# Attention tile: where the sink columns are transposed and copied, and the order of logits and natural transposes

## The chip, the core and the metric

The kernel runs on one core of one Trainium2 chip. The metric is the device time of one execution in microseconds (us). A core has five engines that work at the same time, each through its own list of instructions in order: TensorE (PE; its weight loads are shown apart as PEld), VectorE (DVE), ScalarE (ACT), GpSimd (POOL) and SyncE (SP, which here only issues DMA transfers). An instruction that needs another engine's result waits for that engine's semaphore, and everything behind it in its own list waits too. Operands lie in SBUF; matmuls write to PSUM, eight banks of 2 KB for each of 128 partitions.

## The reference

Attention with a window of 128 keys and 4 sink keys over 4 batches, 8 heads, 768 positions and 64 elements a head; its output, 3072 tokens of 512 elements, goes through a mixture of 16 experts (4 groups of 4, one expert a token).

```python
def _attn_ref(q, k, v, n_sink, window):
    scores = scale * np.matmul(q, k.transpose(0, 1, 3, 2))
    keep = is_sink | in_window          # pos < 4, or 0 <= row - col < 128
    scores = np.where(keep, scores, -1000000000.0)
    scores = scores - np.max(scores, axis=-1, keepdims=True)
    a = np.exp(scores)
    a = a / (np.sum(a, axis=-1, keepdims=True) + 1e-09)
    return np.matmul(a, v)

def _moe_ref(x, w_group, w_expert, w1, w2):
    # per token: group by argmax, then expert of that group by argmax
    h = np.maximum(xg[mask_e] @ w1[g, e], 0.0)
    ye = h @ w2[g, e]
    out[tok_idx] = (g_w * e_w)[:, None] * ye
```

## The kernel before

The 3072 rows are cut into 24 tiles of 128 rows (6 tiles for each of 4 batches); all 8 heads of a tile are worked together. One loop (`for i in range(NI + 2)`) runs the tiles as a pipeline three deep. Cycle `i` does for tile `i` the scores, row maxima and exponentials; for tile `a = i - 1` the transposes of the exponentials, their copies to SBUF, masks, and the product with the values; for tile `b = i - 2` the logits of the router, the transposes back to natural row order, the normalisation (`norm`) and the store of the attention output. After the loop the experts run: gathered rows, two matmul layers, scatter. What fills the gaps of the loop is weight preparation (`whi`, `wlo`) and the routing arithmetic on DVE.

The order on each engine is the order in which the code calls the engine (every call is pinned in program order), so moving a line of the loop moves its instructions on each engine.

The steps that matter here, with the tile names that a profile row shows as `out<-in`:

- `scores(i, 0)` and `scores(i, 1)`: PE writes `ps`, four heads each.
- `trans(a)`: 16 PE transposes of the exponentials, `tp<-ident,pt`, into both banks of the pair `tp`.
- `sink_t(a)`: two PE transposes of the 96 sink columns (4 sinks of 8 heads in three pieces, made by POOL as `sp`), `lg<-ident,sp` and `po<-ident,sp`: they go to the first 64 columns of the two banks `ob[0]` (named lg) and `ob[1]` (named po).
- `evac(a, 0)`, `evac(a, 1)`: ACT copies the two halves of `tp` to SBUF, `pa<-tp`; for every tile that is not the first of its batch POOL then makes two masked versions of each half (`pu<-pa`, `pa<-pa`).
- `sink_evac(a)`: ACT casts the two pieces of transposed sinks, `spT<-lg` and `spT<-po`.
- `maxima(i, g)` on DVE (`sm<-ps,msk`), `exps(i, g)` on ACT (`pt<-sm,st`), four heads each.
- `logits(b)`: PE, `lg<-wsd,xT`; `natural(b)`: 8 PE transposes, `tp<-ident,xT`, into the first half of both `tp` banks; `norm(b)`: DVE, `xt<-tp,rc`.
- `values(a, 0)`, `values(a, 1)`, `sink_values(a)`: PE accumulates into `po` (`po<-pu,vv`, `po<-pa,vv`, `po<-spT,svp`); `out_evac(a)`: ACT copies it, `xT<-po`.

`tp` is one pair of banks for the whole loop (`bufs=1`), so the transposes of cycle `i + 1` wait until `norm(b)` of cycle `i` has read it.

Of the kernel before, what the change touches and what calls it, by code (L numbers as in the profile page):

```python
# [22 lines left out]
B, H, S, D = 4, 8, 768, 64  # L23
# [5 lines left out]
NDC = DM // P  # L29
# [100 lines left out]
def moe_attention(tc, kqT, vN, vS, nsw, wgx, w1, w2, out):  # L130
    nc = Pinned(tc)
    v = nc.vector
    with ExitStack() as top, ExitStack() as att:
# [15 lines left out]
        def const(shape, dt, name):  # L149
            return cp.tile(shape, dt, name=name)  # L150
# [17 lines left out]
        vts, svs, env, bat = {}, {}, {}, {}  # L168
# [4 lines left out]
        def pair():  # L173
            return ps_p.tile([P, 2, 4 * P], F32, name="tp")
# [55 lines left out]
        ident = const([P, P], F32, "ident")  # L230
# [106 lines left out]
        def put_gates(n):  # L337
            for _ in range(min(n, len(gates))):
                t, g = gates.pop(0)
                nc.sync.dma_start(xd[t * P:(t + 1) * P, DM:XW], g)  # L340
# [292 lines left out]
        def gather(r, j):  # L633
            w = min(P, CAPT[r] - j * P)
            cc = BASE[r] + j
            xg[r, j] = t = gp.tile([P, XW], F32, name="xg")
            src = xd[0:sum(BATCHES[:(SNAP if j < EC else SNAPB) + 1]) * P] if r == 0 else xd
            nc.gpsimd.indirect_dma_start(
                out=t[0:w], out_offset=None, in_=src,
                in_offset=bass.IndirectOffsetOnAxis(ap=gidx[0:w, cc:cc + 1], axis=0))  # L640
# [8 lines left out]
        def dve(us):  # L649
            state["dve"] = max(state["dve"], state["clk"]) + us  # L650
# [3 lines left out]
        def prefetch(depth):  # L654
            while len(raws) < depth and state["issued"] < len(chunks):
                l, r, c = chunks[state["issued"]]
                if (f"id{r}" if r < 2 else "eid") not in ready:
                    return
                state["issued"] += 1
                if r not in regs:  # L660
                    src = (eidi if r > 1 else eid01)[0:1, r:r + 1]
                    regs[r] = nc.nc.values_load(src, engines=[ENG.SP], min_val=0, max_val=NE - 1)
                e = bass.ds(regs[r], 1)
                rw = raw()[:, 0:F]
                if l == 1:
                    nc.sync.dma_start(rw, w1[e, c * P:(c + 1) * P, :].rearrange("o p f -> (o p) f"))
                else:
                    nc.sync.dma_start(rw.rearrange("p (k n) -> p k n", k=2),
                                      w2[e, 2 * c * P:(2 * c + 2) * P, :].rearrange("o (k p) n -> p (o k) n", p=P))
                state["dma"] = max(state["dma"], state["clk"] + DMALAG) + DMATIME  # L670
                raws.append((l, r, c, rw, state["dma"] + DMASLACK))

        def wjob(force=False):
            if tail:
                prefetch(RAW)
            k = state["done"]
            if raws and not force and state["clk"] < raws[0][4]:
                return None
            if not raws or k >= state["freed"] + WBUF or (k % WBUF >= WA and len(wpool) < 2):
                return None  # L680
            l, r, c, rw, _ = raws.pop(0)
            wp = wpool[k % WBUF >= WA]
            hi = wp.tile([P, F], F32R, name="whi")
            lo = wp.tile([P, F], F32R, name="wlo")
            z = F if tail else F // 2
            nc.scalar.copy(hi[:, 0:z], rw[:, 0:z])

            def rest():
                v.tensor_tensor(lo, rw, hi.bitcast(F32), ALU.subtract)
                wt[l, r, c] = hi, lo  # L690
                if tail:
                    prefetch(RAW)
            dve(1.2)
            state["done"] += 1
            if tail:
                rest()
                return True

            def more():
                nc.scalar.copy(hi[:, z:], rw[:, z:])  # L700
                return rest

            half.append(more)
            return None

        psb = [ps_s.tile([P, 4, 256], F32, name=f"ps{g}") for g in range(2)]
        ob = [ps_a.tile([P, DM], F32, name=n) for n in ("lg", "po")]
# [74 lines left out]
        def sink_t(i):  # L782
            sp = env[i]["sp"].rearrange("p a h k -> p (a h k)").bitcast(F32)
            for f in range(2):
                r = slice(f * D, (f + 1) * D)
                nc.tensor.transpose(ob[f][0:96, 0:D], sp[r], ident[r, r])

        def sink_evac(i):
            env[i]["spT"] = spT = wk.tile([96, P], F32R, name="spT", bufs=2)
            for f in range(2):  # L790
                nc.scalar.copy(spT[:, f * D:(f + 1) * D], ob[f][0:96, 0:D])

        po = ob[1].rearrange("p (c n) -> p c n", c=HP)
        lg = ob[0][:, D:D + 2 * H * PW].rearrange("p (t n) -> p t n", t=2)
# [25 lines left out]
        def natural(i):  # L820
            for c in range(NDC):
                for j in range(2):
                    r = slice(j * D, (j + 1) * D)
                    nc.tensor.transpose(env["tp"][:, j, c * D:(c + 1) * D], env[i]["xT"][r, c], ident[r, r])

        def logits(i):
            xT = env[i]["xT"]
            for c in range(NDC):
                for g in range(2):
                    r = slice(g * D, (g + 1) * D)  # L830
                    nc.tensor.matmul(lg[r, i % 2, 2 * c * PW:2 * (c + 1) * PW], xT[:, c, r],
                                     wsd[:, c].rearrange("p j n -> p (j n)"), start=True, stop=True)
# [247 lines left out]
        for i in range(NI + 2):  # L1080
            live = i < NI
            a, b = i - 1, i - 2
            mid, old = 0 <= a < NI, 0 <= b < NI
            state["clk"] += 3.0
            if i == NI:
                state.update(gap=0.0, dve=state["clk"])
                sps.close()
                put_gates(MAXB)
                while later:
                    gather(*later.pop(0))  # L1090
                ps_h = fl.enter_context(tc.tile_pool(name="ps_h", bufs=4, space=PSUM, side="right", reuse_waits="tile"))
                tail.append(ps_h)
                next(ew)
                next(ew)
                if half:
                    half.pop()()()
            if live:
                load_v(i)
            if live:
                scores(i, 0)  # L1100
                if i == 1:
                    scores(i, 1)
            if mid or old:
                env["tp"] = pair()
            if mid:
                trans(a)
                sink_t(a)
                evac(a, 0)
                sink_evac(a)
                evac(a, 1)  # L1110
            late = None
            if live:
                if i != 1:
                    scores(i, 1)
                issue()
                warm(FILL[i] if i < len(FILL) else 0, ob[0][:, 224:416])
                late = half.pop()() if half else wjob()
            if live:
                maxima(i, 0)
                exps(i, 0)  # L1120
            else:
                routing(TSTEP, (None,))
                next(ew, None)
            if old:
                logits(b)
                natural(b)
            if live:
                maxima(i, 1)
                exps(i, 1)
                sink_split(i)  # L1130
            if i == 0:
                late_consts()
            if i % NT == (4 if i else 0) and i < NI - NT + (not i):
                split_s((i + 2) // NT)
            state["clk"] += 3.0
            if old:
                norm(b)
            routing(1, ("pe",))
            if old:
                norm_logits(b)  # L1140
            if late:
                late()
            if mid:
                values(a, 0)
                values(a, 1)
                sink_values(a)
                out_evac(a)
            if later and not gates:
                gather(*later.pop(0))
            put_gates(2 if live else MAXB)  # L1150
            routing((REND if i < NI - 1 else 2) if live else TSTEP, (None, "rd"))
            if live and i % 2:
                sums(i)
            if i >= CHOOK and (i % 2 == 0 or i > NI - 4):
                prefetch(min(RAW, len(raws) + (1 if live else RAW)))
            if not live:
                wjob()
                next(ew, None)
# [48 lines left out]
        with tc.If(fv > 0), ExitStack() as fv_pool:  # L1207
            tp = fv_pool.enter_context(tc.tile_pool(name="tabw", bufs=1))
# [233 lines left out]
```

## Time and profile before

| | us |
|---|---|
| median of 3 runs | 518.01 (516.5 to 519.64) |
| the profiled execution | 516.01 |
| its span, first to last instruction | 514.2 |
| busy on DVE, ACT, POOL | 381.9 (74%), 345.1 (67%), 158.8 (31%) |
| 24 executions of `xT<-po` (end of a tile's values) | from 16.3 to 166.2 |

The granted TensorE clock is 0.997 of full speed over the span. The attention loop lies between about 6 and 170 us of the span, the experts behind it. Rows of the view of instructions in order of time read: start (us), length (us), engine, line (here always a recording helper's, L100), operation, out<-in, shape, xcount of merged instructions, and in brackets the engine's idle time before the row and what ended it. Matmuls overlap, so a group's share of PE is the distance from its start to the next group's start, not its length.

### The profile page before, as it was taken

Reading aid. Unit: us, or ns where it says so; the run is one execution under the profiler, and the core shown is the slowest. Engines: PE = TensorE matmul, PEld = TensorE weight load, DVE = VectorE, ACT = ScalarE, POOL = GpSimd, SP = SyncE. Lnnn points to the kernel's source line nnn. Section 1 sums busy time; section 2 is a strip of 40 time slices with the busy share of each in tenths; the row PEclk is TensorE's granted clock in tenths of the full one; section 3 lists DMA queues with packets and bytes.
Section 4 is the critical chain, followed back from the end, with each engine's and each line's share of the span. In section 5 each row is a group of like instructions: output and inputs, shape, how many; then the busy total and the mean of one; then the engine's idle time right before and its main releaser. Section 6 shows DMA issues by size and latency. Waiting matters only on the chain. (4 is left out here: it accounts for less than half of the span.)

```text
span 514.2 us, 14708 instructions
## 1 busy us (share of the span) xinstructions
PE 498.3 (97%) x5399; PEld 418.1 (81%) x5399; DVE 381.9 (74%) x1183; ACT 345.1 (67%) x901; POOL 158.8 (31%) x272
## 2 busy tenths in 40 slices
PE   7999999999899999999999999999999999999994
PEld 5788888878678888989889878787779788988884
DVE  7566986987996889984175668946988887788840
ACT  4888887888875345772274677745877887688631
POOL 3454462453465012423304013121243033202201
PEclk9999999999999999999999999999999999999998
DMA  7777877687786545896239488859878896779200
GB/s 199 245 212 215 235 213 221 216 320 212 221 291 153 181 123 205 303 319 227 67 92 319 130 267 313 277 163 297 283 246 307 305 319 226 263 244 321 93 24 27
DMA packets 50000, 114.33 MB, mean 222 GB/s; under 512 B 9486, under 2 KB 9486, under 8 KB 49920
## 3 DMA queue, kind: packets, MB, share of 16 engines
q1 hardware_dynamic: 45424, 99.96, 60.3%
q0 software_dynamic: 4352, 13.06, 7.2%
q8 instruction: 44, 0.72, 0.6%
q10 hardware_dynamic: 144, 0.29, 0.3%
q14 instruction: 36, 0.29, 0.2%
HBM read 100.69 MB, written 13.05 MB: 221 GB/s over the span
## 5 line engine op out<-in xcount | busy, mean ns | idle before, releaser
L100 DVE TENSOR_TENSOR wlo<-rw,whi 128x1024 fp32r<-128x1024 f32 x128 | 153.2, 1219 | 36.4 <-ACT whi L100 36.1
L100 PE MATMUL po<-whi,un 128*128 128x512 f32 (+3 forms) x448 | 149.2, 393 | 0.0
L100 ACT CAST whi<-rw 128x1024 fp32r<-128x1024 f32 (+1 forms) x132 | 131.7, 1023 | 18.2 <-DMA rw<-in_w 15.2
L100 PE MATMUL ph<-un,whi 128*128 128x256 f32 (+4 forms) x576 | 132.2, 317 | 1.1 <-DVE un L100 0.6
L100 POOL DMA_INDIRECT out<-ot,sidx x33 | 45.5, 1380 | 236.0 <-ACT ot L100 142.3
L100 PE MATMUL po<-wlo,un 128*128 128x512 f32 (+4 forms) x264 | 101.6, 390 | 0.0
L100 PE MATMUL ph<-un,wlo 128*128 128x160 f32 (+4 forms) x416 | 100.6, 267 | 0.0
L100 PEld LDWEIGHTS po<-whi,un 128*128 128x128 f32 (+2 forms) x448 | 79.9, 179 | 23.6
L100 PEld LDWEIGHTS ph<-un,whi 128*128 128x128 f32 x576 | 94.8, 189 | 3.5 <-DVE hc L100 1.0
L100 ACT ACTIVATE pt<-sm,st 128x136 f32<-128x136 f32 x192 | 75.8, 407 | 9.8 <-DVE st L100 9.8
L100 PEld LDWEIGHTS ph<-un,wlo 128*128 128x128 f32 x416 | 77.2, 189 | 0.8
L100 PEld LDWEIGHTS po<-wlo,un 128*128 128x128 f32 (+3 forms) x264 | 43.5, 165 | 13.2
L100 DVE CUSTOM_DVE_ANT_0 sm<-ps,msk 128x136 f32<-128x136 f32 x192 | 45.9, 295 | 6.7 <-PE ps L100 2.2
L100 PE MATMUL ps<-kb,qb 64*64 64x216 f32 (+1 forms) x768 | 44.7, 351 | 2.0 <-DMA qb<-in_kqT 2.0
L100 POOL DMA_INDIRECT xg<-xd,gidx x33 | 35.0, 1061 | 32.9 <-DVE idz L100 20.9
L100 ACT ACTIVATE ot<-po,cg 128x512 f32<-128x512 f32 (+4 forms) x33 | 22.5, 681 | 31.6 <-PE po L100 22.7
L100 DVE TENSOR_TENSOR hc<-ph,hc 128x160 f32<-128x160 f32 (+2 forms) x64 | 22.1, 346 | 23.4 <-ACT hc L100 23.3
L100 ACT ACTIVATE un<-ph 128x256 fp32r<-128x256 f32 (+1 forms) x40 | 15.7, 395 | 34.2 <-PE ph L100 33.7
L100 ACT COPY pa<-tp 128x512 f32<-128x512 f32 x48 | 28.5, 593 | 15.0 <-PE po L100 13.6
L100 ACT ACTIVATION_READ_ACCUMULATOR pt<-sm,st 128x1 f32 x192 | 38.2, 199 | 0.0
L100 POOL TENSOR_SCALAR_AFFINE_SELECT pu<-pa 64x512 f32<-64x512 f32 x40 | 26.4, 660 | 22.0 <-ACT pa L100 18.1
L100 ACT COPY hc<-ph 128x160 f32<-128x160 f32 (+2 forms) x64 | 19.8, 311 | 19.2 <-PE ph L100 11.8
(190 smaller groups left out, 723.8 us busy)
## 6 DMA issues: line engine op xcount, KB each, us to landing
rw<-in_w SPq DMA_DIRECT2D x128, 512.0 KB, 4.9
vv<-in_vN SPq DMA_DIRECT2D x24, 512.0 KB, 5.0
kb<-in_kqT SPq DMA_DIRECT2D x23, 288.0 KB, 4.6
qb<-in_kqT SPq DMA_DIRECT2D x24, 256.0 KB, 4.0
xd<-xt SPq DMA_DIRECT2D x24, 256.0 KB, 3.9
svr<-in_vS SPq DMA_DIRECT2D x4, 192.0 KB, 4.9
xg<-xd,gidx POOLq DMA_INDIRECT x33, 4.5
out<-ot,sidx POOLq DMA_INDIRECT x33, 5.0
```

The costliest lines, as they stand in the source:

```text
L100: r = f(*a, **k)
```

## The change

The two sink transposes leave their place behind `trans(a)` and go behind `scores(i, 1)`; they write columns 256 to 319 of the two `tp` banks and not `lg` and `po`. One cast takes both pieces from there, and it stands on ACT between `exps(i, 0)` and `exps(i, 1)`. `natural(b)` and `logits(b)` change places, and both move ahead of `maxima(i, 0)` in the code, so that on PE they stand directly behind the sink transposes (nothing of `maxima` or `exps` is on PE).

```diff
         def sink_t(i):
@@
-                nc.tensor.transpose(ob[f][0:96, 0:D], sp[r], ident[r, r])
+                nc.tensor.transpose(env["tp"][0:96, f, NDC * D:(NDC + 1) * D], sp[r], ident[r, r])

         def sink_evac(i):
             env[i]["spT"] = spT = wk.tile([96, P], F32R, name="spT", bufs=2)
-            for f in range(2):
-                nc.scalar.copy(spT[:, f * D:(f + 1) * D], ob[f][0:96, 0:D])
+            nc.scalar.copy(spT.rearrange("p (f q) -> p f q", f=2), env["tp"][0:96, :, NDC * D:(NDC + 1) * D])
@@
             if mid:
                 trans(a)
-                sink_t(a)
                 evac(a, 0)
-                sink_evac(a)
                 evac(a, 1)
@@
                 late = half.pop()() if half else wjob()
+            if mid:
+                sink_t(a)
+            if old:
+                natural(b)
+                logits(b)
             if live:
                 maxima(i, 0)
                 exps(i, 0)
             else:
                 routing(TSTEP, (None,))
                 next(ew, None)
-            if old:
-                logits(b)
-                natural(b)
+            if mid:
+                sink_evac(a)
             if live:
                 maxima(i, 1)
                 exps(i, 1)
```

On PE, one cycle from the steady part of the loop (`-` is before, `+` now):

```order
 L100 MATMUL ps_195<-kb,qb 64x216 x8
 L100 MATMUL tp<-ident,pt 128x64 x16
-L100 MATMUL lg<-ident,sp 96x64
-L100 MATMUL po<-ident,sp 96x64
 L100 MATMUL ps_196<-kb,qb 64x216 x8
-L100 MATMUL lg<-wsd,xT 64x40 x8
-L100 MATMUL tp<-ident,xT 128x64 x8
+L100 MATMUL tp<-ident,sp 96x64 x2
+L100 MATMUL tp<-ident,xT 128x64 x8
+L100 MATMUL lg<-wsd,xT 64x40 x8
 L100 MATMUL po<-pu_109,vv 64x64 x8
 L100 MATMUL po<-pa,vv 64x64 x8
```

The sink transposes now stand next to the natural transposes, and the logits next to the values.

On ACT, the same cycle before, from one copy of a finished tile to the exponentials:

```order
L100 COPY xT<-po 128x512
L100 COPY pa<-tp 128x2x4x64
L100 CAST spT<-lg 96x64
L100 CAST spT<-po 96x64
L100 COPY pa<-tp 128x2x4x64
L100 ACTIVATE pt,st<-sm,st 128x2x68 x8
```

And now, the same stretch:

```order
L100 COPY xT<-po 128x512
L100 COPY pa<-tp 128x2x4x64 x2
L100 ACTIVATE pt,st<-sm,st 128x2x68 x4
L100 CAST spT<-tp 96x128
L100 ACTIVATE pt,st<-sm,st 128x2x68 x4
```

The two casts that stood between the two copies are one cast, behind four of the eight exponentials.

On DVE, around `norm(b)` in a cycle of the same part, with what each instruction waits for:

```order
 L100 ISA sm,st<-ps_196,msk 128x136
 L100 ISA st 128x1
-L100 TENSOR_TENSOR xt<-tp,rc 128x2x4x64 [waits DMAHW7_49,PE_49,Activation_49]
-L100 TENSOR_TENSOR lw<-lg,rc 128x320
+L100 TENSOR_TENSOR xt<-tp,rc 128x2x4x64 [waits DMAHW7_49,Activation_49]
+L100 TENSOR_TENSOR lw<-lg,rc 128x320 [waits PE_49]
 L100 TENSOR_REDUCE lt<-lw 128x40 [waits DVE_49]
```

No DVE instruction has moved, but `norm(b)` now waits for ACT alone (an ACT instruction that itself comes behind the natural transposes: the cast), and the product with the logits waits for PE on its own.

## The prediction

> **What bounds the kernel now.** I read the page first, then the stretches of the attention loop and of the experts, then one steady cycle on each engine, and last the waits within the loop.
>
> ```profile
> span 514.2 us, 14708 instructions
> PE 498.3 (97%) x5399; PEld 418.1 (81%) x5399; DVE 381.9 (74%) x1183; ACT 345.1 (67%) x901; POOL 158.8 (31%) x272
> ...
> 10.00:158.20 148.20, 144.20 (x3185) 116.76 (x3173) 118.46 (x589) 122.50 (x507) 73.53 (x185) 1.00 0.77 235
> ```
>
> The last line is the loop: its length, then the busy time of PE, PEld, DVE, ACT and POOL. PE is busy for 144.2 of 148.2 us, and nearly all the time behind it, so a shift of PE's stream in the loop reaches the end almost whole. But "busy" hides how the cycle is held. Here is one steady cycle (tile 10) on PE:
>
> ```profile
> 66.71 0.71 PE L100 MATMUL tp<-ident,pt 64*128 64x64 f32 x16
> 67.25 0.22 PE L100 MATMUL lg<-ident,sp 64*96 64x64 f32 x1
> ...
> 67.40 0.96 PE L100 MATMUL ps<-kb,qb 64*64 64x216 f32 x16
> 68.29 0.67 PE L100 MATMUL lg<-wsd,xT 128*64 128x40 f32 x16
> 68.89 0.46 PE L100 MATMUL tp<-ident,xT 64*128 64x64 f32 x8
> 69.28 0.69 PE L100 MATMUL po<-pu,vv 128*64 128x64 f32 x16
> 69.80 0.64 PE L100 MATMUL po<-pa,vv 128*64 128x64 f32 x16
> 70.26 0.66 PE L100 MATMUL po<-pu,vv 128*64 128x64 f32 x16
> 70.95 0.69 PE L100 MATMUL po<-pa,vv 128*64 128x64 f32 x16
> 71.57 0.66 PE L100 MATMUL po<-spT,svp 96*128 96x128 f32 x4
> ```
>
> From start to start: transposes 0.54, sinks 0.15, scores 0.89, logits 0.60, natural transposes 0.39, then values 0.52, 0.46, 0.69, 0.62. The third block of values takes 0.69 where its like takes 0.46: PE waits there about 0.2 for the last mask. POOL makes the four masks in a row as soon as ACT has copied the first half:
>
> ```profile
> 67.54 0.59 ACT L100 COPY pa<-tp 128x512 f32<-128x512 f32 x1 [0.97 <-PE po L100]
> 68.02 0.21 ACT L100 CAST spT<-lg 96x64 fp32r<-96x64 f32 x1
> ...
> 68.23 0.60 ACT L100 COPY pa<-tp 128x512 f32<-128x512 f32 x1
> ...
> 68.19 0.65 POOL L100 TENSOR_SCALAR_AFFINE_SELECT pu<-pa 64x512 f32<-64x512 f32 x1 [1.91 <-ACT pa L100]
> ...
> 70.25 0.65 POOL L100 TENSOR_SCALAR_AFFINE_SELECT pa<-pa 64x512 f32<-64x512 f32 x1
> ...
> PEld po L100 <- POOL pa L100: 2.1, 12, 0.2
> ```
>
> The first mask begins when the first copy ends (67.54 + 0.59), the fourth ends at 70.90, and PE goes on at 70.95. The last line counts the waits of this kind in the loop: 12, together 2.1 us. So in 12 of the cycles the ring transposes, first copy, masks, last values, next transposes sets the pace, with PE 0.2 us ahead of it; elsewhere it is PE alone (first tiles of a batch, which have no masks, and cycles with routing matmuls ahead of the values).
>
> **The change part by part, on PE.** Without the sinks behind the transposes, the second scores start 0.06 earlier (67.34), and the sinks could start at 67.34 + 0.89 = 68.23. They write the `tp` banks, so they wait for both copies out of them. The second copy takes the place of the first cast, 68.02, and ends at 68.62. How soon PE resumes is shown where the logits wait for a cast:
>
> ```profile
> 81.01 0.21 ACT L100 CAST spT<-lg 96x64 fp32r<-96x64 f32 x1
> ...
> 81.27 0.32 PE L100 MATMUL lg<-wsd,xT 128*64 128x40 f32 x4 [0.15 <-ACT spT L100]
> ```
>
> That is 0.05 after the cast's end at 81.22. So the sinks start at 68.67, with PE idle for 0.44, a wait that the logits filled before. These rows show another thing: the logits waited for a cast out of other columns of the same bank, so bank neighbours are kept apart. The Trainium skill ("PSUM — Partial Sum Buffer", PSUM bank collisions raise a hardware error) says that any two engines, two readers too, are to be kept apart by bank and not by address; the trace agrees (the 0.05 above). By addresses alone `norm` would not wait for the cast, and my sum below would be about 1.2 lower (no delay in cycles 7, 13 and 19).
>
> From the sinks on: sinks and natural transposes with the switch behind them 0.06 + 0.18 + 0.15 = 0.39, logits 0.44 without their switch (0.60 - 0.16), 0.05 into the values, which follow with no switch between: values at 69.55, against 69.28, **0.27 later**. With no switch ahead, the first block takes 0.47: the fourth block is ready at 69.55 + 3 x 0.47 = 70.96. The masks allow it at 70.95. In the 12 cycles the old wait for the mask just covers the new one for the copy: I count **0 for each**, between -0.05 (the fourth block starts without a restart) and +0.11. The upper end is a second copy that begins when the first has ended (0.59 behind its start) and not 0.48 behind it, as the cast does; the trace has no two such copies in a row, and I take the cast's row as the nearest.
>
> The switches: a group of another tile shape costs 0.15 (behind 64-column work) to 0.27 (behind scores) at its start against 0.05 within a shape. The change has one switch fewer a cycle. The Trainium skill ("TensorEngine Tiling (Array Packing)", Key Properties) says that changing the tiling mode drains the array; the rows agree. If that were all, every cycle would gain about 0.13; that is a rival below.
>
> **Cycles without cover.** Cycle 2 gains. There the sinks held PE for POOL's pieces:
>
> ```profile
> 16.23 0.71 PE L100 MATMUL tp<-ident,pt 64*128 64x64 f32 x16
> 17.18 0.26 PE L100 MATMUL lg<-ident,sp 64*96 64x64 f32 x1 [0.24 <-POOL sp L100]
> ...
> 19.85 0.69 PE L100 MATMUL po<-pu,vv 128*64 128x64 f32 x16
> ```
>
> Now the scores start at 16.87, the dummy matmuls at 17.76, the sinks at 18.36, when both copies are done; values at 18.36 + 0.88 = 19.24, 0.61 earlier, and 0.05 more without the switch. Cycle 1 loses 0.08, since its sinks' values wait for the cast behind four exponentials. Together **-0.6**.
>
> Cycles 11 and 18 have routing matmuls between transposes and values, so the masks are done in time:
>
> ```profile
> 73.05 0.71 PE L100 MATMUL tp<-ident,pt 64*128 64x64 f32 x16
> ...
> 75.63 0.88 PE L100 MATMUL lg<-af,bf 128*128 128x112 f32 x6
> 76.43 0.69 PE L100 MATMUL po<-pu,vv 128*64 128x64 f32 x16
> ```
>
> Sinks at 73.05 + 1.96 = 75.01, logits done by 75.84, a switch 0.16, routing 0.80: values at 76.80 for 76.43, 0.37 each, **+0.7**.
>
> **The cast behind the exponentials.** It is queued on ACT behind four exponentials, and `norm` on DVE waits for it. Behind `norm` on DVE stand the routing and the next maxima. In cycle 7 the fifth exponential begins at 52.06; without the two casts ahead (0.21) the new cast starts at 51.85 and, costed between the 0.21 of a 96x64 cast and the 0.59 of a 128x512 copy, near the small one, takes 0.26: `norm` at 52.16.
>
> ```profile
> 51.79 0.69 DVE L100 TENSOR_TENSOR xt<-tp,rc 128x512 f32<-128x512 f32 x1
> ...
> 52.06 0.41 ACT L100 ACTIVATE pt<-sm,st 128x136 f32<-128x136 f32 x1
> ...
> 58.58 0.39 ACT L100 ACTIVATE pt<-sm,st 128x136 f32<-128x136 f32 x1
> ...
> 58.88 0.66 PE L100 MATMUL po<-spT,svp 96*128 96x128 f32 x4
> ```
>
> That is 0.38 late, and DVE has no gap from there to the maxima of cycle 8. So the fifth exponential of cycle 8 moves from 58.58 to 58.96, its cast ends at 59.22, and the sinks' values start at 59.27 for 58.88: +0.39 for cycles 7 and 8 (the switch path alone gives 0.27). Cycles 13 and 14 are built alike, +0.3. Together **+0.7**. In steady cycles DVE has room and the same delay costs nothing.
>
> Cycles 19 to 21 are the worst, since a weight copy (0.52) stands ahead of the exponentials:
>
> ```profile
> 127.91 0.68 DVE L100 TENSOR_TENSOR xt<-tp,rc 128x512 f32<-128x512 f32 x1
> ...
> 128.82 0.40 ACT L100 ACTIVATE pt<-sm,st 128x136 f32<-128x136 f32 x1
> ...
> 127.50:141.40 13.90, 13.06 (x60) 1.00 0.76 235
> ...
> 139.47 1.15 POOL L100 DMA_INDIRECT xg<-xd,gidx  x1 [0.87 <-DVE ps L100]
> ...
> 141.37 0.69 PE L100 MATMUL po<-pu,vv 128*64 128x64 f32 x16 [0.58 <-POOL pu L100]
> ```
>
> The cast ends at 128.82 - 0.21 + 0.26 = 128.87, `norm` starts at 128.92 and not 127.91: 1.0 later. The third line is DVE alone: busy for 13.06 of 13.90 us, so nothing takes the delay up. The gather on POOL waits for DVE's work (or the store behind it), and the masks and PE wait for the gather: **+1.0**, with 0 as the lower end if the gather hangs on something earlier. PE's own losses up to there (0.3 to 0.6) vanish in that wait.
>
> **The end of the loop.** In cycle 24 PE waits for the second copy as well, while the expert work that it did meanwhile comes later: +0.25. In cycle 25 the natural transposes come ahead of an expert block, so `norm` no longer waits 0.40, and PE's later wait of 0.80 for DVE shrinks with it:
>
> ```profile
> 170.04 0.69 DVE L100 TENSOR_TENSOR xt<-tp,rc 128x512 f32<-128x512 f32 x1 [0.40 <-PE tp L100]
> ...
> 175.29 0.66 PE L100 MATMUL ph<-ident,xg 128*128 128x128 f32 x4 [0.80 <-DVE un L100]
> ```
>
> Together **-0.1**. Sum: -0.6 + 0.7 + 0.7 + 1.0 - 0.1 = **+1.7 us**. The profiled execution took 516.01, 1.8 more than its span and 2.0 below the median of 518.01; it would become 517.7, and the median **519.7**.
>
> **The rivals.**
> 1. Slower: the second copy comes later than I count. The 12 covered cycles have no slack left (70.96 against 70.95), so each 0.1 us between the copies' end and the sinks costs there at once, and in the 4 uncovered ones too. At 0.2 us (0.11 for copies that do not overlap, the rest in the resumption) that is 16 x 0.2 = 3.2: 522.9. For it: nothing in the trace shows the pair of copies; against it: the cast follows a copy at 0.48.
> 2. The DVE delay is taken up: the gather does not depend on `norm`. Then 518.7.
> 3. Faster: the switches alone count, since the copies end in time. Four uncovered cycles gain 0.13 each and not 0.3, the sinks' stalls for POOL (six waits before) go, about -3.0 in all: 515.0. Against it stands the row of the second copy: it would have to end 0.4 us earlier. By the skill's tiling page alone this would be the outcome.
>
> **How the numbers follow.** My forecast has 0.55, rival 2 0.13, rival 1 0.25, rival 3 0.07. Less than 0.5% (2.6 us) can't be told from no change here. Forecast and rival 2 lie within it; of the forecast a sixth of its chance falls above it, since 519.7 is near the bound of 520.6. That gives faster 0.06, same 0.60, slower 0.34. The range: the low end takes the 12 cycles at -0.05 (-0.6), no DVE term (-1.0), and the 1.5 by which runs lie below their median: 516.6; the high end is rival 1 with a little of the spread: 523.2.
>
> **What would show it.** Right: sinks 1.9 to 2.0 us behind the start of the transposes, behind a PE gap of about 0.4; the 12 waits for masks nearly gone; cycles of the steady part still 6.35 long; `norm` waiting for ACT, by about 1 us where a weight copy stands ahead. Wrong: steady cycles of 6.5 or more (rival 1), or below 6.3 (rival 3), or the tile-21 values at the old distance from tile 19 (rival 2).

## The result, and the profile after

The changed kernel took 523.39 us (median of 4 runs, 521.77 to 524.16) beside 517.25 us for the kernel before on the same chip: a ratio of 1.0107, with a 95% interval of 1.0063 to 1.0151. Measured once more beside others (first experiment below) it took 519.99 for 517.49, ratio 1.0062 [1.0027, 1.0096]. It is slower, by 0.6 to 1.1%. The forecast was 519.7, slower by 0.3%, with a range up to 523.2: the first median lies 0.2 us above that range, the second within it. The medians are of all executions and the ratios leave out the few in a slower state, and a ratio is not the quotient of the two medians beside it (519.99 / 517.49 is 1.0048).

The head of the page after, to be read against the one before:

```profile
span 520.1 us, 14651 instructions
PE 494.1 (95%) x5399; PEld 416.0 (80%) x5399; DVE 382.4 (74%) x1183; ACT 343.3 (66%) x877; POOL 158.4 (30%) x272
```

The span grew by 5.9 us while PE's busy time fell by 4.2: the work did not grow, PE waits more. The view by stretches shows the loop again (length, busy time of PE, PEld, DVE, ACT, POOL, then the granted clock):

```profile
10.00:165.20 155.20, 140.75 (x3185) 114.87 (x3174) 118.75 (x587) 121.41 (x483) 75.57 (x185) 0.99 0.74 225
```

It is 7.0 us longer than before's 148.2, and PE is idle in it for 14.4 us and not for 4.0. The view of what the engines waited for in the loop (us in total, times, longest):

```profile
DVE xt L100 <- ACT spT L100: 11.5, 18, 1.3
PE tp L100 <- ACT pa L100: 10.6, 21, 1.1
...
PE ps L100 <- issue: 1.7, 1, 1.7
...
PEld po L100 <- POOL pa L100: 0.3, 2, 0.2
```

The first line is `norm` waiting for the cast, as foreseen, the second PE's new wait for the second copy. The third is a stall for which the profile has no releaser. The last is what is left of the twelve waits for masks, 2.1 us before. PE's groups and the copies of one steady cycle (tile 10) after, in order of time:

```profile
67.35 0.71 PE L100 MATMUL tp<-ident,pt 64*128 64x64 f32 x16
67.99 0.96 PE L100 MATMUL ps<-kb,qb 64*64 64x216 f32 x16
68.18 1.07 ACT L100 COPY pa<-tp 128x512 f32<-128x512 f32 x2 [0.97 <-PE tp L100]
69.40 0.26 PE L100 MATMUL tp<-ident,sp 64*96 64x64 f32 x2 [0.45 <-ACT pa L100]
69.47 0.44 PE L100 MATMUL tp<-ident,xT 64*128 64x64 f32 x8
69.84 0.67 PE L100 MATMUL lg<-wsd,xT 128*64 128x40 f32 x16
70.33 0.66 PE L100 MATMUL po<-pu,vv 128*64 128x64 f32 x16
...
71.76 0.64 PE L100 MATMUL po<-pa,vv 128*64 128x64 f32 x16
...
73.81 0.71 PE L100 MATMUL tp<-ident,pt 64*128 64x64 f32 x16
```

Both copies end at 68.18 + 1.07 = 69.25, as costed (the second 0.48 behind the first). But the sinks begin at 69.40, 0.15 behind that and not 0.05, and 2.05 behind the transposes and not 1.96. The values begin 2.98 behind the transposes; I had 2.84, before had 2.57. From the sinks to the values PE takes 0.93, where sinks, logits and natural transposes took 0.15 + 0.60 + 0.39 = 1.14 before: the switch of tile shape that the change saves is there. The cycle is 6.46 long and was 6.34. The prediction had named 6.35 as the sign of its being right and 6.5 or more as that of rival 1; this lies between the two, nearer to rival 1.

The stall without a releaser is in cycle 15, first on PE, then in stretches of 2 us:

```profile
105.82 0.76 PE L100 MATMUL ps<-kb,qb 64*64 64x216 f32 x9
108.31 0.89 PE L100 MATMUL ps<-kb,qb 64*64 64x216 f32 x7 [1.74 <-issue]
109.13 1.12 PE L100 MATMUL tp<-ident,pt 64*128 64x64 f32 x16
```

```profile
106.00:108.00 2.00, 0.58 (x9) 0.16 (x5) 1.46 (x9) 0.57 (x1) 0.12 (x1) 1.00 0.92 332
108.00:110.00 2.00, 1.69 (x23) 1.07 (x23) 0.72 (x4) 0.00 (x0) 0.00 (x0) 0.62 0.75 293
110.00:112.00 2.00, 2.00 (x28) 1.03 (x24) 0.71 (x9) 1.63 (x4) 0.90 (x2) 0.53 0.02 8
```

PE stands still for 1.74 us amid one group of matmuls whose operands were there for the ones before it; behind that the granted clock is 0.62 and 0.53 in two stretches of 2 us (from 108.5 to 111.9 it is 0.50), so the next transposes take 1.12 for 0.71. My prediction had no such term.

### The profile page after: what moved, and what is told of

It reads as the page before. It is cut to its first block, busy times and chain, and to the rows that moved or that the text cites. A ratio compares the mean times of both kernels' runs of the same rounds, so it can differ in the third digit from the quotient of the medians.

```text
span 520.1 us, 14651 instructions
## 1 busy us (share of the span) xinstructions
PE 494.1 (95%) x5399; PEld 416.0 (80%) x5399; DVE 382.4 (74%) x1183; ACT 343.3 (66%) x877; POOL 158.4 (30%) x272
## 3 DMA queue, kind: packets, MB, share of 16 engines
HBM read 100.69 MB, written 13.05 MB: 219 GB/s over the span
## 5 line engine op out<-in xcount | busy, mean ns | idle before, releaser
L100 PE MATMUL ph<-un,wlo 128*128 128x160 f32 (+4 forms) x416 | 100.6, 267 | 0.0
L100 PE MATMUL ps<-kb,qb 64*64 64x216 f32 (+1 forms) x768 | 46.2, 358 | 3.7 <-DMA qb<-in_kqT 2.0
L100 POOL DMA_INDIRECT xg<-xd,gidx x33 | 32.7, 990 | 33.2 <-DVE idz L100 20.6
L100 ACT COPY pa<-tp 128x512 f32<-128x512 f32 x48 | 25.8, 589 | 20.1 <-PE tp L100 19.9
L100 PEld LDWEIGHTS ps<-kb,qb 64*64 64x64 f32 x768 | 25.5, 137 | 10.3 <-issue 4.4
```

What stands on the lines that cost most here:

```text
L100: r = f(*a, **k)
```

## Theories and a table of all runs

- **Theory 1**: PE waits for the second copy ahead of the sinks; the logits, now behind, no longer fill that time. **1a**: 0.1 of it comes from a wait on two engines at once.
- **Theory 2**: the cast behind four exponentials holds `norm` on DVE, and through it the routing, the gathers and the next exponentials.
- **Theory 3**: the stall at cycle 15 is a late fetch of PE's own instructions, which hangs on where the blocks of instructions end and not on the order of the work.

All twelve runs, with the lengths of cycles in their profiled executions (us, from the last transpose of the exponentials in a cycle to the last in the next; the heads 10, 7-8 and so on are the numbers of the cycles; "fetch" is the sum of the stalls of theory 3, found as told under the first experiment; "behind" is from cycle 24 to the end). Times are medians beside 517.49 (e1 to e4), 518.03 (e5 to e8) and 517.17 us (e9 to e12) for the kernel before.

```
run              us     ratio [95%]             10    7-8    11   13-14  15-17  18   19-21 fetch behind
before         517.25                          6.34  11.87  6.65  12.06  19.75 6.87 20.80  1.08  355.5
after          523.39 1.0107 [1.0063,1.0151]   6.45  12.42  7.16  12.86  22.19 7.40 21.71  2.37  354.4
e1 after again 519.99 1.0062 [1.0027,1.0096]   6.45  12.42  7.15  12.86  22.22 7.40 21.71  2.33  354.5
e2 lg,sink,nat 519.19 1.0026 [0.9985,1.0066]   6.35  13.05  6.63  12.75  22.22 7.25 21.72  2.66  353.9
e3 nat,sink,lg 516.57 0.9978 [0.9944,1.0013]   6.37  12.24  7.06  12.40  19.03 7.31 21.72  0     353.9
e4 cast on DVE 518.82 1.0032 [0.9998,1.0065]   6.45  12.42  7.16  12.57  22.83 7.40 21.12  3.00  354.0
e5 after+64    521.68 1.0064 [1.0037,1.0091]   6.53  12.42  7.37  12.59  19.13 7.39 21.73  3.80  355.6
e6 before+64   517.93 0.9999 [0.9965,1.0034]   6.35  11.87  6.64  12.96  19.31 7.25 20.79  3.04  355.3
e7 lg,nat,sink 518.09 1.0021 [0.9994,1.0048]   6.34  13.04  6.64  13.05  19.00 7.04 21.71  0     355.3
e8 e3+DVE cast 518.41 1.0011 [0.9986,1.0036]   6.37  12.78  7.06  12.40  18.98 7.31 21.06  0.84  353.7
e9 e3+early    518.17 1.0031 [1.0007,1.0054]   6.37  12.35  7.06  12.51  21.77 7.48 20.89  2.16  353.6
e10 weights    521.38 1.0091 [1.0061,1.0122]   6.45  12.42  7.16  12.59  19.13 7.40 21.73  0     356.5
e11 e3 again   517.57 1.0011 [0.9995,1.0027]   6.37  12.24  7.06  12.40  19.04 7.31 21.85  0     355.1
e12 e7+DVE     516.53 0.9987 [0.9964,1.0010]   6.35  12.15  6.64  12.15  18.99 6.71 20.91  0.88  352.7
```

Cycle 22 is not in the table. It took 6.35 in the kernel before and 6.54 in e1, but 7.19 in the first profile of the changed kernel, where ACT began the first copy 0.65 later behind the same transposes; in e3 and e7 to e12 it took 6.97 to 7.18. What held the copy stays open.

## Experiment 1: the changed kernel again

> The changed kernel once more, nothing altered. In its first profile the tensor engine stood still for 1.74 us amid a group of scores of cycle 15 with no releaser ("issue") and ran at a granted clock of 0.53 to 0.62 behind it; cycle 15 took 9.19 us where its like take 6.45. Theory A (a stroke of one execution, or of where a block of instructions is fetched while the DMA engines are full): the stall is absent, or of another length, and the profiled time is 518.5 to 520.5. Theory B (it belongs to the changed order): the stall comes at the same place with 1.5 to 2.0 us, and the profiled time is 521 to 523. By both, steady cycles are 6.45 and the ratio to the kernel before is 1.005 to 1.015.

The stall came at the same matmul, with the same length (2.06 us from matmul to matmul, for 2.08), and every cycle up to 14 had the same length to 0.02. By its place alone theory B stood. What it is, I read from the trace's DMA records: one queue is marked "instruction" and carries 44 packets of 16384 bytes for PE's 10,922 recorded instructions: some 256 to a packet, 64 bytes each. Counted back from the stall in steps of 256 recorded instructions (a few records may be missing), these are the fetches in the trace:

```
kernel  block   block ahead begins   packet moved    block runs from   packet's end to block   PE stalls
after   14       95.1                 98.3 +1.0       100.5             1.2                      0.29
after   15      100.5                105.9 +0.9       108.3             1.5                      2.08
after   16      108.3                109.4 +1.3       114.5             3.8                      0
before  16      103.6                106.9 +0.9       109.3             1.5                      0.33
before  17      109.3                113.4 +0.9       115.8             1.5                      0.75
```

At all but 12 of 347 edges in the fourteen profiles up to 165 us, a block's packet moved after the block ahead of it had begun (at those 12 at most 1.0 us before). No block of the loop ran sooner than 1.1 us behind its packet's end. At 26 edges with 1.2 to 1.7 us between the two PE paused, for 0.17 to 2.47 us (at 18 others with so little it did not); where the packet came earlier, the pause is at most 0.35. These 26 I count as stalls. All 26 stand in front of the same place in the count (recorded instruction 193 modulo 256), whatever work is there. The kernel before has two of them, which the views in my prediction did not set apart from PE's work. The Trainium skill ("Runtime: NRT & Kernel Launch", Instruction fetch mechanics) says that instructions are fetched in blocks of 16 KiB, 256 of them, and that the cost of a block's edge is mostly hidden. The size agrees with the 16384 bytes here, and most edges show no pause; but at 26 the cost was not hidden. Here PE used up the block that began at 95.1 in 5.4 us, and the packet that moved only 5.4 us after the block ahead of it had begun (105.9 for 100.5) cost 2 us.

## Experiments 2 to 4: one part of the change each

Experiment 2 puts the logits ahead:

```diff
+            if old:
+                logits(b)
             if mid:
                 sink_t(a)
             if old:
                 natural(b)
-                logits(b)
```

> The changed kernel with the logits ahead of the sinks and the natural transposes, so that they fill the time until the second copy ends. Theory 1 (the loss is the tensor engine's wait for the second copy): the waits for that copy, 10.6 us in 21 stretches of the changed kernel, fall below 1.5 us; steady cycles go from 6.45 to 6.35, with the wait for the last mask back at 0.2; cycles 11 and 18 give back 0.4 each; the time is 3 to 4 us below the changed kernel. Theory 2 (the loss is the cast behind four exponentials, which holds norm on the vector engine): steady cycles as said, but the loss in cycles 7, 13 and 19 to 21 stays, and the time is at most 1.5 us below the changed kernel. By both together: 2 us below the changed kernel, ratio to the kernel before 1.002 to 1.007.

PE's waits for the copy fell from 10.6 us to none in the view of waits, steady cycles to 6.35, cycle 11 to 6.63: theory 1 held in each of these. The time did not follow: 0.8 us below the changed kernel, less than the intervals can tell. The fetch stall stayed (2.66 in all), and cycles 7 and 8 grew from 12.42 to 13.05, by a mechanism that experiment 7 shows.

Experiment 3 puts the natural transposes ahead of the sinks:

```diff
+            if old:
+                natural(b)
             if mid:
                 sink_t(a)
             if old:
-                natural(b)
                 logits(b)
```

> The changed kernel with the natural transposes ahead of the sinks. The first instruction behind the scores then waits for the scalar engine alone, and not for the scalar engine and GpSimd at once. Theory 1a (the sinks resume 0.114 us behind the copy, and not 0.05, since a wait for two engines takes an instruction of its own): the natural transposes start 0.05 to 0.07 behind the copy's end, values start 0.06 earlier, steady cycles are 6.38 to 6.40, the time is about 1 us below the changed kernel. Theory 1b (0.11 is what any such wait takes): nothing moves, steady cycles 6.45, time within 0.5 us.

The same place in a steady cycle of this kernel:

```profile
67.56 1.07 ACT L100 COPY pa<-tp 128x512 f32<-128x512 f32 x2 [0.97 <-PE tp L100]
68.68 0.46 PE L100 MATMUL tp<-ident,xT 64*128 64x64 f32 x8 [0.35 <-ACT pa L100]
68.98 0.22 PE L100 MATMUL tp<-ident,sp 64*96 64x64 f32 x2
```

The copies end at 68.63, the natural transposes begin 0.05 later, where the sinks took 0.15: theory 1a. Steady cycles are 6.37, the unmasked cycle 7 (5.44 for 5.52) and cycle 11 gained 0.08 to 0.1 as well. The trace has 96 semaphore instructions on PE for 119 in the changed kernel, one less a cycle: the sinks waited for ACT (the banks) and for POOL (the pieces `sp`). The Trainium skill ("Perfetto Trace Analysis", Identifying Dependency Chains) says that an instruction that waits on several engines may get a semaphore instruction ahead of it; the trace agrees, and here it costs 0.08 to 0.10 a cycle. A rival would be the sinks' own tile shape, which in the changed kernel comes first behind the scores and here does not. The kernel before rules it out, where the same transposes wait for POOL alone:

```profile
131.06 0.25 POOL L100 TENSOR_TENSOR sp<-pt,sp 128x32 fp32r<-128x32 f32 x1
...
131.36 0.26 PE L100 MATMUL lg<-ident,sp 64*96 64x64 f32 x1 [0.54 <-POOL sp L100]
```

They begin 0.05 behind POOL's end (131.31), and 0.05 to 0.06 in all six such waits of that profile. The time, 3.4 us below the changed kernel, was more than a tenth a cycle can give (24 x 0.1). The profile of this order has no fetch stall; that this is the rest is not shown.

Experiment 4 moves the cast alone:

```diff
-            nc.scalar.copy(spT.rearrange("p (f q) -> p f q", f=2), env["tp"][0:96, :, NDC * D:(NDC + 1) * D])
+            v.tensor_copy(spT.rearrange("p (f q) -> p f q", f=2), env["tp"][0:96, :, NDC * D:(NDC + 1) * D])
...
                 exps(i, 0)
...
-            if mid:
-                sink_evac(a)
             if live:
...
+            if mid:
+                sink_evac(a)
             if old:
                 norm(b)
```

> The changed kernel with the cast of the sinks done by the vector engine just ahead of norm, and not by the scalar engine behind four exponentials. Theory 1 (the wait for the second copy is the loss): steady cycles stay 6.45, time within 1 us of the changed kernel. Theory 2 (the late cast holds norm): cycles 7 and 8 together, 13 and 14 together and 19 to 21 give back 0.3, 0.3 and 0.9; the time is 1.5 to 2 us below the changed kernel, while the vector engine's busy time rises by about 5 us (24 casts of 0.2).

Mixed for theory 2. Cycles 19 to 21 gave back 0.6 (21.12 for 21.71), but cycles 7 and 8 nothing (12.42), although the exponentials of cycle 8 started 0.7 earlier. Cycles 13 and 14 took 12.57, which is what they take with the late cast where no fetch stall falls into them (12.59 in e5 and e10). So in cycles 7, 8, 13 and 14 the cast was not the bound. The time was 1.2 us below the changed kernel, less than the 1.5 to 2 expected by theory 2.

## Experiments 5, 6 and 10: the fetch

Experiments 5 and 6 add the same lines to the changed kernel and to the kernel before:

```diff
         warm(WARM)
+        dst = pair()[:, 0, 0:32]
+        for _ in range(32):
+            nc.tensor.matmul(dst, wz[:, 0:P], wz[:, 0:32], start=True, stop=True)
```

> The changed kernel with 32 dummy matmuls of 32 columns (64 instructions of the tensor engine) more at its start, where that engine waits some 2 us for the first load. In the traces so far the tensor engine's instructions come in packets of 16384 bytes, 256 instructions, one fetched whenever a block of 256 has been begun; the stall of 2.0 to 2.5 us came at the same instruction (number 4289 of the trace) in all four kernels that had it, and the fetch for it waited 5.4 us in full DMA queues. Theory A (the stall is a fetch that comes late, by where the block's edge falls against the loads): the edges fall 64 instructions (about 1.4 us) earlier in the work, the stall at cycle 15 is gone or below 0.8 us, cycle 15 takes 6.45 to 7.2 and not 9.2, the profiled span is 516.5 to 518.5 for 519.6 to 520.1. Theory B (the stall belongs to the changed order of the work in cycle 15): it stays at 1.7 to 2.1 us amid the second half of cycle 15, span 519.5 to 520.5.

> The kernel before with the same 64 instructions more at its start. In its own profile two fetches came late, at 0.33 and 0.75 us of stall in cycles 16 and 17. Theory A: these stalls move or change by up to 2 us in either direction, while steady cycles stay 6.35; the time may change by -1 to +3 us against the kernel before although the work is the same. Theory B: stalls and time as before, within 0.5 us.

With the edges of the blocks 64 instructions earlier, the stall at cycle 15 is gone and cycle 15 takes 6.45, the steady length. It came back elsewhere: six smaller ones, the last of them here, amid a group in cycle 23,

```profile
161.63 0.63 PE L100 MATMUL po<-pa,vv 128*64 128x64 f32 x14
163.39 0.27 PE L100 MATMUL po<-pa,vv 128*64 128x64 f32 x1 [1.13 <-issue]
```

together 3.80 us, and the span of 521.2 was 2.7 us above the upper end of what theory A expected. So theory 3 is shown for the place (it follows the blocks' edges, not the work), and my guess that there would then be less of them was wrong. The kernel before with its edges moved has 3.04 us of stalls in its profile, for 1.08, and the same median as without. The two shifted profiles have about the same stalls (3.80 and 3.04), and the ratios are 1.0064 against 0.9999: as far as the profiles stand for the other executions, the change loses time beside the stalls.

Experiment 10 sets the cycle from which the loop asks for weights (`CHOOK`) from 14 to 16.

> The changed kernel with the first weight loads of the loop asked for from cycle 16 on and not from cycle 14; nothing else is altered. Theory A (the fetch of the tensor engine's instructions waits behind the loads in the DMA queues): the DMA engines are less full from 100 to 106 us, and the stall at cycle 15 falls from 2.1 to below 0.7 us, or moves behind cycle 16; cycle 15 takes 6.45 to 7.1. Theory B (the fetch's lateness has nothing to do with the loads): the stall stays at 1.7 to 2.1 us. The time is 518 to 520 by theory A, unless the stall comes back later.

No fetch stall at all; cycle 15 took 6.46. The time, 521.38, missed the 518 to 520. But this doesn't show what I had put as the cause: the DMA engines moved 216 GB/s from 98.3 to 105.9 us for 183 in the changed kernel, so they were not less full, and in the changed kernel they had been idle from about 100.6 to 102.3 while block 15 was outstanding. What the packet of 105.9 waited for stays open; no record shows when it is asked for. So the "full DMA queues" of my expectation were not shown to be the cause. Of the 2.3 us gained in the loop, 2.0 were lost behind it (356.5 for 354.5), where PE now waits 0.8 for a prepared weight (`wlo`).

## Experiments 7 to 9, 11 and 12: both costs away

Experiment 7 has the order logits, natural transposes, sinks; experiment 12 the same with the cast on DVE as in experiment 4.

> The changed kernel with the order logits, natural transposes, sinks behind the second scores: the logits fill the time until the second copy ends, and the first instruction that needs the copies waits for one engine. Theory 1 (the wait for the copy is what the change costs in the loop): no wait of the tensor engine for that copy, steady cycles 6.35, cycles 7, 13 and 11 at 5.14, 5.14 and 6.65 as in the kernel before; the loss against the kernel before up to cycle 14 goes from 1.8 us to under 0.5. Theory 2 (the late cast costs on its own): cycles 19 to 21 still take 21.7 us together, for 20.8 before, and the time stays about 1 us above where it would be. The stall of the instruction fetch is open: 0 to 2.5 us. Time 515 to 518.5 for 517.5 before.

Steady cycle of experiment 7:

```profile
67.87 0.71 PE L100 MATMUL tp<-ident,pt 64*128 64x64 f32 x16
68.51 0.96 PE L100 MATMUL ps<-kb,qb 64*64 64x216 f32 x16
68.70 1.07 ACT L100 COPY pa<-tp 128x512 f32<-128x512 f32 x2 [0.97 <-PE tp L100]
...
69.40 0.67 PE L100 MATMUL lg<-wsd,xT 128*64 128x40 f32 x16
69.99 0.46 PE L100 MATMUL tp<-ident,xT 64*128 64x64 f32 x8
...
71.42 0.65 PE L100 MATMUL po<-pu,vv 128*64 128x64 f32 x16
72.11 0.69 PE L100 MATMUL po<-pa,vv 128*64 128x64 f32 x16
...
74.21 0.71 PE L100 MATMUL tp<-ident,pt 64*128 64x64 f32 x16
```

No wait for the copies, and the old wait for the last mask is back (the fourth block 0.69 behind the third). From cycle 3 to 7 the kernel runs as the one before, and in cycles 11 and 13 too (6.64 for 6.65, 5.15 for 5.14). But cycles 8 and 14 take 7.89 each, for 6.73 and 6.91, and the waits of PE are now

```profile
PE po L100 <- ACT spT L100: 2.9, 5, 1.0
PE lg L100 <- DVE oh L100: 2.1, 3, 1.4
```

In cycle 8 the routing on DVE runs into POOL's masks:

```profile
54.95 0.28 DVE L100 TENSOR_REDUCE rm<-req 128x30 f32<-128x120 f32 x1
55.09 0.65 POOL L100 TENSOR_SCALAR_AFFINE_SELECT pu<-pa 64x512 f32<-64x512 f32 x1 [0.80 <-ACT pa L100]
...
55.26 0.62 DVE L100 TENSOR_TENSOR req<-req,rm 128x120 f32<-128x120 f32 x1
...
55.81 0.65 POOL L100 TENSOR_SCALAR_AFFINE_SELECT pa<-pa 64x512 f32<-64x512 f32 x1
55.91 0.66 DVE L100 TENSOR_TENSOR oh<-req 128x96 bf16<-128x96 f32 x1
...
56.42 0.66 POOL L100 TENSOR_SCALAR_AFFINE_SELECT pu<-pa 64x512 f32<-64x512 f32 x1
56.49 0.62 DVE L100 TENSOR_SCALAR rc<-st 128x16 f32<-128x16 f32 x1
```

Each of `req`, `oh` and `rc` begins within a mask here and ends 0.03 to 0.14 behind that mask's end. In the kernel before only `oh` did (0.58); `req` and `rc` began just ahead of a mask and took 0.28 and 0.16, for 0.62 each here. Not every operation is held: the reciprocal and the copies under a predicate behind them begin within masks too (in the kernel before at 55.98 and 56.15, in the mask of 55.83) and keep their 0.25 and 0.41. The exponentials start 1.2 us later in the cycle than there, the cast behind them, and the sinks' values wait 1.0 for it. So theory 2 is real in cycles 8 and 14 too (experiment 12, with the cast on DVE, gives back 0.9 of 7-8 and of 13-14), but in the changed kernel PE, held by the copies, arrives late enough not to see it.

One more loss lies in cycle 20 of this kernel and of experiments 3 and 11: the granted clock is 0.50 for 3.4 us (136.4 to 139.8 here) without a fetch stall, behind waits of PE of 1.0 to 1.4 us for the routing on DVE. The cycle took 9.5 there, for 8.45 in the changed kernel; but 19 to 21 together took the same 21.7 (21.85 in experiment 11), since cycle 21 was shorter by as much.

Experiment 8 is experiment 3 with the cast on DVE, experiment 9 experiment 3 with the cast ahead of the first exponentials, experiment 11 experiment 3 again.

> The natural transposes ahead of the sinks, and the cast of the sinks on the vector engine just ahead of norm. Theory 1: steady cycles 6.37 as without the cast's move. Theory 2: cycles 19 to 22 take 0.6 to 1.3 us less than the 28.8 us that they take with the cast on the scalar engine; time 515.3 to 516 for 516.6. By theory 1 alone the cast's move changes nothing beyond 0.3 us.

> The natural transposes ahead of the sinks, and the cast of the sinks on the scalar engine ahead of the first four exponentials and not behind them. The cast then comes at about 2.0 us into a cycle, and the exponentials start at 2.3 for 1.3. Theory 2 (the late cast holds norm, and through it the gathers of cycles 19 to 22): norm no longer waits for the scalar engine, cycles 19 to 22 take 27.2 to 27.8 us together as in the kernel before (27.15), for 28.8 with the late cast, and the time is 1 to 1.5 us below that version (515.1 to 515.6 where it takes 516.6). Rival (the exponentials, now 0.9 later, become the bound): cycles 7 and 13, the short ones, grow by 0.2 to 0.6 each and the time is the same or up to 1 us longer. By both, steady cycles stay 6.37.

> The natural transposes ahead of the sinks, once more, to tell its time from the kernel before. First theory (its 516.57 for 517.49 came from fetch stalls that it does not have and the others do): ratio 0.996 to 1.000 again, steady cycles 6.37, no fetch stall above 0.5 us. Second theory (chance): ratio 1.000 to 1.004, with stalls of 0.5 us and more in the profiled execution.

> Logits, natural transposes, sinks, and the cast of the sinks on the vector engine ahead of norm: neither the wait for the copy nor the late cast on the scalar engine. Theories 1 and 2 together: steady cycles 6.35, cycles 7 and 13 5.14, cycles 19 to 22 27.2 to 28 us, the profiled span about 513.5 to 515.5 without fetch stalls, time 515 to 516.5. Rival: the sinks' values wait for the cast behind the maxima in cycles 8, 14 and 20, about 1 us each, as they did with the cast on the scalar engine in this order (7.89 each for 6.73 and 6.91); then 517 to 518.5.

Theory 2 held in cycles 19 to 21: 21.06 with the cast on DVE, 20.89 with the early cast, 20.80 before, 21.7 with the late cast. This is the `norm` of cycle 19, first in the changed kernel, then with the early cast:

```profile
133.73 0.25 ACT L100 CAST spT<-tp 96x128 fp32r<-96x128 f32 x1
134.01 0.69 DVE L100 TENSOR_TENSOR xt<-tp,rc 128x512 f32<-128x512 f32 x1 [0.95 <-ACT spT L100]
```

```profile
132.46 0.26 ACT L100 CAST spT<-tp 96x128 fp32r<-96x128 f32 x1
133.07 0.69 DVE L100 TENSOR_TENSOR xt<-tp,rc 128x512 f32<-128x512 f32 x1
```

It waits 0.95 in the one and not in the other. Yet neither time gained: e8 was expected at 516 or less and took 518.41, e9 at 515.6 or less and took 518.17, with a fetch stall of 2.16 us in cycle 17,

```profile
117.29 0.63 PE L100 MATMUL po<-pu,vv 128*64 128x64 f32 x14
119.86 0.22 PE L100 MATMUL po<-pu,vv 128*64 128x64 f32 x1 [1.94 <-issue]
```

and a start that was 1.2 us later. The rival for e9, that cycles 7 and 13 grow, came to 0.05 each. The repeat of experiment 3 gave 1.0011 where it had given 0.9978: no gain over the kernel before that a measurement can tell, although its profile again has no fetch stall, as the first theory had it. Experiment 12, with neither the wait nor the late cast in a steady cycle, has the shortest profile of all:

```profile
span 512.3 us, 14687 instructions
```

Cycles 7 and 8 take 12.15, 18 takes 6.71 and 19 to 21 take 20.91 (its rival shows in cycle 20, where the sinks' values wait 1.14, and in 8 and 14 with 0.5 and 0.4). Its time, 516.53 for 517.17, is a ratio of 0.9987 [0.9964, 1.0010]. That interval lies below the changed kernel's [1.0027, 1.0096], so with both costs away the loss is gone; and nothing found here beats the kernel before by more than its spread.

## Why the prediction was off: its steps

The direction of the sum was right, its size not: +1.7 us, where the second measurement shows 0.62% of 517.5, that is +3.2, and the first +6.1. The largest chance, 0.60, lay on less than 0.5% of a difference, and both measured ratios are above that (the second one's interval reaches below it). By stretches of the profiles (e1 less before):

```
step                              predicted   in the profiles
cycles 1 and 2                      -0.6       -0.44
twelve cycles covered by masks       0         +0.87 (eight), +0.46 (15 to 17, fetch taken off), +0.19 (22)
cycles 11 and 18                    +0.7       +1.03
cycles 7, 8, 13, 14                 +0.7       +1.08 (fetch stall of 0.27 taken off)
cycles 19 to 21                     +1.0       +0.91
behind cycle 24                     -0.1       -1.0
sum without the fetch               +1.7       +3.1
```

For cycles 15 to 17 the +0.46 is 19.13 (experiments 5 and 10, which have neither a stall nor the slow clock there) less 18.67 (the kernel before without its 1.08 of stalls). That +3.1 and the measured +3.2 agree so well is in part chance: for experiment 3 the spans with the stalls taken off give +1.7, where its two measurements gave -0.22% (-1.1 us) and +0.11% (+0.6).

- **The covered cycles: the step that failed.** "In the 12 cycles the old wait for the mask just covers the new one for the copy: I count 0 for each, between -0.05 [...] and +0.11." It was +0.11, the upper end, in the steady ones: the term put at 0 came to +1.5 over the twelve. The reason given for that end (copies that don't overlap) was not it: the copies ran as counted. The 0.05 for PE's resumption came from a wait for one engine, and the sinks wait for two: 0.15 (experiment 3 brings it back to 0.05, and the cycle to 6.37). Rival 1 had the form right (no slack left, so each 0.1 ahead of the sinks costs at once), but about half its size.
- **Cycles 11 and 18**: right mechanism, too small by the same 0.1 and some 0.05 each; experiments 2 and 7 take the loss away in cycle 11.
- **Cycles 7, 8, 13, 14**: right sign, wrong cause, so that the +0.7 came near the +1.08 was luck. I had the delayed `norm` as the larger of two paths (0.39 against 0.27). It was the path of PE itself, 0.4 late in cycle 7 and 0.2 more in 8; experiment 4 takes the cast away from ACT and gains nothing there. The delay of `norm` lay beside it, hidden, and shows at 1.0 where PE's wait is taken away (experiment 7).
- **Cycles 19 to 21**: right, in cause and size: experiments 4, 8 and 9 give back 0.6 to 0.8 of 0.9. Rival 2 (the gather doesn't hang on `norm`) fell.
- **Rival 3**: the switch saved is real (0.93 for 1.14 in a steady cycle), but the waits for copies, 10.6 us, swallowed it.
- **Behind the loop**: -1.0 is not explained. That stretch took 352.7 to 355.6 in the profiles of kernels that leave it alone, so it is within what the profiles vary by.
- **Not in the sum at all: the fetch of instructions.** The profile of the kernel before that I summed against (516.0 us) has 1.1 us of stalls; other executions have more, as its median of 517.5 and experiment 6 suggest. The changed kernel's profiles have 2.3 to 2.4, and about 1 us of slow clock behind (22.22 - 2.06 - 19.13 in cycles 15 to 17 of e1). 3.1 + (2.33 - 1.08) + 1.03 is the 5.4 by which e1's span exceeds before's, where the medians of the second measurement differ by 2.5. How many stalls an execution without a profile has is not shown.

## What to carry over

Where a new wait just fits under an old one, its price is the whole of what was rounded: take the resumption from a row with the same number of engines waited for, and if the end of the range costs a dozen cycles at once, forecast nearer to it. Two delays that lie beside each other hide each other: taking one away (experiments 2 and 7, ratios 1.0026 and 1.0021) gained less than taking away both (experiment 12, 0.9987), though these three intervals overlap. And before a shift of one us is argued from one execution, look for stalls that the profile calls "issue" amid a group of matmuls, in the kernel before too: they move with anything that changes the count of PE's instructions, and a single one cost 2 us here.

## What the hardware showed that was not expected

- PE's instructions arrive in packets of 16384 bytes, and a block ran no sooner than 1.1 us behind its packet's end; 26 stalls of 0.17 to 2.47 us in fourteen profiles, all at the same place of the count modulo 256.
- After the stall of 2 us the granted clock was 0.50 for 3.4 us (108.5 to 111.9); in experiments 3, 7 and 11 it was 0.50 for 3.4 us in cycle 20, where PE's longest wait had been 1.0 to 1.4 us.
- A wait for two engines resumed PE 0.15 us behind the later one, a wait for one engine 0.05.
- A TENSOR_SCALAR of 0.16 us and a TENSOR_TENSOR of 0.28 us on DVE took 0.62 when they began within one of POOL's masks; a reciprocal of 0.25 and a predicated copy of 0.41 did not grow.
